# The value products of four quadrants in one TensorE stage, with constants, loads, early experts and a planner's table re-ordered

## The chip, the cores and the metric

The kernel runs on one core of a Trainium2 chip. The metric is device time in microseconds (us) for one execution; lower is better. Five engines work side by side and each takes its instructions strictly in the order of its own list: PE (TensorE, matrix products), DVE (VectorE), ACT (ScalarE), POOL (GpSimd) and SP, which here only issues transfers. POOL issues transfers too.

## What is computed

First a two-part attention over q, k, v of shape 8 x 8 heads x 576 x 64; then its output, as 4608 rows of 512, goes through a mixture of 8 experts, of which every row takes the one with the largest gate.

```python
# attention: a coarse part on means over 4 positions, and a local part
q_d, k_d, v_d = (t.reshape(B, H, S // 4, 4, D).mean(axis=3) for t in (q, k, v))
out_up = np.repeat(sm_attn(q_d, k_d, v_d), 4, axis=2)
mask = np.abs(pos[:, None] - pos[None, :]) < 4
out_local = softmax(np.where(mask, scale * q @ k.T, -1e9)) @ v
x = (out_up + out_local) as rows [4608, 512]
# experts
e_idx = argmax(x @ w_gate, axis=1); gate_w = the largest softmax value
eom = sigmoid(x @ w_output_gate)
out[row] = gate_w[row] * eom[row, e] * (relu(x[row] @ w1[e]) @ w2[e])   # e = e_idx[row]
```

## The kernel before, in words

**Attention.** The work is cut into 32 head pairs (8 batches of 4 pairs), called units `u`. Each runs the same stages: `prep` transposes q and k on PE (L450) and multiplies them with scaled identities for the means (L457, with `idq` and `idk`); DVE and ACT take the results out of PSUM (`qT` L465, `qd` L471, `kT` L478, `kd` L485). `vm` makes the means of v on PE (L497). `scores` does the coarse scores `ms` (L515), a mask product (L524) and the local scores `ls` (L533, 48 small products), then one exponential on ACT (L539), the only one of that line, so that 32 runs of L539 count the units. `values` makes numerators and denominators `uden` (L558, L560, L563), a logarithm and an exponential on ACT (L570, L572), the normalised local weights `en` on POOL (L574), `um` on DVE (L582), and then the local values `val` on PE (L596): 24 products for quadrants 0 and 1 of the sequence into one PSUM pair, then 24 for quadrants 2 and 3 into another. A float32 product stands in the trace as two rows, so a unit has 96 rows of L596. DVE adds both parts into `xT` (L604), POOL casts them (L609).

**Gate.** After each batch `gate` works out the expert and the slot of every row (L641 to L738), and six indirect transfers from POOL scatter the rows into `hx_xs`, sorted by expert (L758).

**Experts.** Each expert has 5 tiles of 128 rows. A `unit` of one or two tiles loads its rows (L808), transposes them (`xgT`, L818, copied by DVE at L822), multiplies with w1 (`up`, L835), applies relu on ACT or DVE (L787, L789), multiplies with w2 (`down`, L850), scales on ACT (L858) and scatters to the output (L792). A two-tile unit has 32 rows of L835 and 16 of L850. `EARLY` names units that may run while attention still goes on: for each of experts 0 to 3 a two-tile unit once the rows of batches 0 to 3 are scattered, and a one-tile unit after batch 5, 12 tiles in all; 28 tiles come after the last batch.

**What sets the order.** Every stage is a task with an engine, a duration, dependences and a priority. `Plan.emit` takes the tasks by earliest start in its own model and writes them out; the engines' lists are the order in which it took them. Wrong durations in that model can't break the result, only make a list wait: `ldv` is planned with 0.06 us on SP, for instance. The constants (L359 to L426) are written out ahead of all tasks. PSUM has four pairs of banks: banks 0 and 1 (`r_T`) for `prep`, `vm` and the gate, three pairs (`r_P`) for scores, `uden` and `val`, and early experts share banks 7 and 6 (`r_Y`) with them; late experts may use all eight (`r_A`).

**First loads.** POOL issues q and k for half a batch (2 units) at a time (L291), SP issues v in 8 transfers of 48 KB for a unit (L320), and 8 fills of `hx_xs` (L869).

Of the kernel before, what the change touches and what calls it, by code (L numbers as in the profile page):

```python
# [16 lines left out]
NGB = 6  # L17
# [6 lines left out]
NJ = 6  # L24
CAPJ = 5
EARLY = {0: ((3, 2), (5, 1)), 1: ((3, 2), (5, 1)), 2: ((3, 2), (5, 1)), 3: ((3, 2), (5, 1))}
LATE_ORDER = (0, 4, 1, 5, 2, 6, 3, 7)
W_AT = (2, 6, 10, 14, 22)
NBLK = 27
Q_AHEAD = 7  # L30
# [8 lines left out]
    "exp_pe": 60.0, "exp_ev": 40.0, "wt": 0.0,  # L39
}  # L40
# [29 lines left out]
class Task:  # L70

    def __init__(self, eng, dur, fn, deps, uses, prio, mode, lat, cost, name):
        self.eng, self.dur, self.fn, self.deps = eng, dur, fn, deps
        self.uses, self.prio, self.mode, self.lat = uses, prio, mode, lat
        self.cost, self.name = cost, name
        self.begin = self.end = self.done = None


class Plan:

    HOP = 0.2
    SWITCH = 0.1

    def __init__(self):
        self.tasks = []
        self.fixed = {}
        self.log = []
        self.dma = 0.0
        self.owner = {}
        self.seen = {}  # L90

    def add(self, eng, dur, fn, deps=(), uses=(), prio=0.0, mode=None, lat=0.0, cost=0.0, name=""):
        t = Task(eng, dur, fn, [d for d in deps if d is not None], list(uses), prio, mode, lat, cost, name)
# [4 lines left out]

    def emit(self, run=True):
        free, mode = {}, None  # L100
        todo = {}
        for t in self.tasks:
            todo.setdefault(t.eng, []).append(t)
        for eng in todo:
            todo[eng].sort(key=lambda t: t.prio)
        n = len(self.tasks)
        while n:
            best = None
            for eng, ts in todo.items():
                here = None  # L110
                at0 = free.get(eng, 0.0)
                for t in ts:
                    s = self.start(t, at0, mode)
# [10 lines left out]
            k, s, t = best  # L124
            if t.mode is not None:
# [3 lines left out]
            t.begin, t.end = s, s + t.dur  # L129
# [5 lines left out]
            todo[t.eng].remove(t)  # L135
            for b in t.uses:
                if b.tile is None:
                    if isinstance(b.ring, Banks):
                        b.banks = self.choose(b, t)[1]
                        for x in b.banks:  # L140
                            self.owner[x] = b
                        b.tile = b.ring.view(b.banks) if run else True
                    else:
# [6 lines left out]
            if run:  # L150
                t.fn()
# [4 lines left out]
    def start(self, t, at, mode):  # L156
        for d in t.deps:
            if d.done is None:
                return None
            at = max(at, d.done + (self.HOP if d.eng != t.eng else 0.0))  # L160
        for b in t.uses:
            if isinstance(b.ring, Banks):
                if b.tile is not None and not b.ring.psum:
                    continue
# [838 lines left out]
```

## Time and profile before

| | |
|---|---|
| median of 3 runs | 593.38 us (584.59 to 598.02) |
| the profiled execution | 592.64 us, its span 590.9 us |
| mean granted TensorE clock | 0.837 of full speed |
| PE busy | 470.2 us (80% of the span) |
| DVE, ACT, POOL busy | 174.7, 142.9, 184.7 us |
| data moved | 65.18 MB, mean 110 GB/s |

The span runs from the first to the last instruction of the profiled execution, which was 592.64 us long. Busy time of PE is read with care: products are pipelined, and the end of each is modelled.

### The profile page before, as it was taken

The numbers are of one execution on the slowest core, as the hardware profiler recorded it, in microseconds if no ns is written. First come the engines' busy times: TensorE is split into PE (matmuls) and PEld (weight loads), VectorE is DVE, ScalarE is ACT, GpSimd is POOL, SyncE is SP. The second block draws the span as 40 slices with busy tenths as digits, with TensorE's granted clock in tenths as the row PEclk, the third lists the DMA queues.
The fourth block names the chain that finished last, engine by engine and source line by source line (L and its number), as shares of the span: only waits on it lengthen the run. The fifth ranks groups of instructions, "written<-read, shape, count | busy, mean of one in ns | idle before, by whom it ended". The sixth has DMA issues, their size and how long they took to land.

```text
span 590.9 us, 22803 instructions
## 1 busy us (share of the span) xinstructions
PE 470.2 (80%) x10283; PEld 364.3 (62%) x10283; DVE 174.7 (30%) x480; ACT 142.9 (24%) x297; POOL 184.7 (31%) x240
## 2 busy tenths in 40 slices
PE   0269987798989968898888788898876878998882
PEld 0157866676877856776757465776754555565651
DVE  3022224313322431532623243225252122131220
ACT  1013122212222222232233322222221222323220
POOL 7002231621532442431442226213424322222211
PEclk9999978557565686767799999658799999999997
DMA  4966997497577574645476356552413584222211
GB/s 55 168 182 111 212 212 121 91 150 111 110 117 126 123 122 82 129 73 119 97 140 145 72 101 119 121 93 33 84 42 116 99 175 109 87 88 81 81 59 55
DMA packets 96430, 65.18 MB, mean 110 GB/s; under 512 B 60737, under 2 KB 88385, under 8 KB 96324
## 3 DMA queue, kind: packets, MB, share of 16 engines
q0 software_dynamic: 31136, 40.43, 36.7%
q1 hardware_dynamic: 65188, 23.20, 17.9%
q8 instruction: 83, 1.36, 1.0%
q14 instruction: 23, 0.19, 0.1%
HBM read 70.33 MB, written 20.53 MB: 154 GB/s over the span
## 4 chain that ended last, share of the span: by engine, by line
PE 71%; issue 9%; DVE 6%; DMA 5%; ACT 5%; POOL 1%; SPq 1%; DVEq 0%; POOLq 0%; ACTq 0%
PE P L835 12%; PE P L850 11%; PE P L596 10%; PE P L558 7%; PE P L563 6%; PE P L450 5%; PE P L457 5%; PE P L497 4%; DMA v<-in_v_dram 3%; PE P L641 2%; PE P L748 2%; ACT hs L787 2%; DVE kT L478 1%; PE P L515 1%; PE P L533 1%
## 5 line engine op out<-in xcount | busy, mean ns | idle before, releaser
L835 PE MATMUL P<-xgT,blk 128*128 128x256 f16 (+1 forms) x768 | 80.0, 256 | 25.1 <-ACT hs L787 11.1
L835 PEld LDWEIGHTS <-blk 128*128 128x128 f16 x768 | 65.0, 98 | 38.0 <-issue 30.4
L850 PE MATMUL P<-blk,hs 128*128 128x512 f16 x320 | 75.1, 379 | 7.9 <-DVE hs L789 4.4
L792 POOL DMA_INDIRECT out_dram<-y,xg x40 | 39.8, 995 | 121.3 <-ACT y L858 117.2
L596 PE MATMUL P<-en,v 32*64 32x24 f32 x3072 | 68.8, 241 | 5.9 <-issue 5.9
L596 PEld LDWEIGHTS P<-en,v 32*64 32x64 f32 x3072 | 62.8, 168 | 15.9 <-issue 13.7
L574 POOL TENSOR_TENSOR en<-e,r 128x288 f32<-128x288 f32 x32 | 25.3, 792 | 120.8 <-issue 72.5
L850 PEld LDWEIGHTS <-hs 128*128 128x128 f16 x320 | 30.5, 98 | 42.3 <-issue 7.2
L450 PE MATMUL P<-id,blk 72*64 72x72 f16 x1024 | 39.8, 238 | 19.1 <-DMA blk<-in_q_dram 11.0
L758 POOL DMA_INDIRECT hx_xs<-xh,g_pos x48 | 45.1, 939 | 31.5 <-DVE g_ohc L708 18.4
L789 DVE TENSOR_SCALAR hs<-P 128x512 f16<-128x512 f32 x40 | 27.7, 692 | 89.7 <-PE P L835 71.2
L609 POOL CAST x<-xT 128x576 f16<-128x576 f32 x32 | 21.3, 666 | 103.6 <-DVE xT L604 86.1
L604 DVE TENSOR_TENSOR xT<-P,u 128x288 f32<-128x288 f32 x64 | 28.9, 455 | 78.1 <-PE P L596 77.5
L558 PE MATMUL P<-e,vd 64*64 64x72 f32 (+1 forms) x512 | 48.2, 351 | 3.6 <-issue 2.2
L450 PEld LDWEIGHTS <-blk 72*64 72x64 f16 x1024 | 32.4, 143 | 27.9 <-issue 15.0
L560 PE MATMUL P<-e,on_d 64*64 64x72 f32 (+1 forms) x512 | 48.6, 351 | 0.0
L858 ACT ACTIVATE y<-P,xg 128x512 f32<-128x512 f32 x40 | 26.8, 686 | 87.6 <-PE P L850 71.7
L497 PE MATMUL P<-v,pv 128*32 128x192 f32 x256 | 28.8, 429 | 21.8 <-DMA v<-in_v_dram 15.2
L558 PEld LDWEIGHTS P<-e,vd 64*64 64x64 f32 x512 | 41.3, 193 | 6.8 <-issue 1.9
L478 DVE COPY kT<-P 128x576 f16<-128x576 f16 x32 | 24.2, 756 | 64.4 <-PE P L457 41.4
L560 PEld LDWEIGHTS P<-e,on_d 64*64 64x64 f32 x512 | 41.7, 193 | 1.2 <-issue 1.2
L563 PE MATMUL P<-e,on_b 128*128 128x144 f32 x128 | 37.8, 441 | 3.2 <-issue 3.2
(118 smaller groups left out, 565.0 us busy)
## 6 DMA issues: line engine op xcount, KB each, us to landing
blk<-in_moe_w_dram POOLq DMA_DIRECT2D x32, 512.0 KB
v<-in_v_dram SPq DMA_DIRECT2D x254, 48.0 KB
hx_xs<-zt SPq DMA_DIRECT2D x8, 645.0 KB
blk<-in_q_dram POOLq DMA_DIRECT2D x15, 288.0 KB
blk<-in_k_dram POOLq DMA_DIRECT2D x15, 288.0 KB
xg<-hx_xs SPq DMA_DIRECT2D x16, 258.0 KB
xg<-hx_xs SPq DMA_DIRECT2D x8, 129.0 KB
hx_xs<-xh,g_pos POOLq DMA_INDIRECT x48
```

The costliest lines, as they stand in the source:

```text
L450: nc.tensor.transpose(t16[64 * h:64 * h + 64, c:c + HB], v_qk(src.tile)[:, h0 + h, a:a + D], id16[0:HB, 0:HB])
L457: nc.tensor.matmul(t32[64 * h:64 * h + 64, c:c + nw], lhsT=v_qk(src.tile)[:, h0 + h, a:a + D], rhs=(idq if i == 0 else idk), start=(m == 0 ...
L478: nc.vector.tensor_copy(kT.tile[:, 4:4 + S].rearrange("p (n j m) -> p n j m", j=2, m=4), T.tile.bitcast(F16)[:, 0:S].rearrange("p (m j n) ...
L497: nc.tensor.matmul(T.tile[r0:r0 + 32, 0:3 * D], lhsT=pv, rhs=vbuf.tile[:, s::2, h, :], start=True, stop=True, skip_group_check=True)
L558: nc.tensor.matmul(p[r, 1, LC + q0:LC + q0 + w], lhsT=vd.tile[r, blk, :], rhs=et[r, i, c0:c0 + w], start=(blk == 0), stop=(blk == 2), skip ...
L560: nc.tensor.matmul(p[rr, 0, DL - SD + q0:DL - SD + q0 + w], lhsT=on_d[r, :], rhs=et[r, i, c0:c0 + w], start=(blk == 0), stop=(blk == 2), s ...
L563: nc.tensor.matmul(p[:, h, DL * (1 - h):DL * (1 - h) + LC], lhsT=on_b, rhs=et[:, h, 0:LC], start=True, stop=True, skip_group_check=True)
L596: nc.tensor.matmul(p[64 * h:64 * h + 64, i, c:c + 24], lhsT=vbuf.tile[r, g, h, :], rhs=et[r, h, 24 * g:24 * g + 24], start=True, stop=True ...
L758: ins = nc.gpsimd.indirect_dma_start(out=xs_dram.ap(), out_offset=bass.IndirectOffsetOnAxis(ap=pos()[:, j:j + 1], axis=0), in_=xh.tile[:, ...
L792: ins = nc.gpsimd.indirect_dma_start(out=out, out_offset=bass.IndirectOffsetOnAxis(ap=idx, axis=0), in_=yt, in_offset=None, bounds_check=N ...
L835: nc.tensor.matmul(o, lhsT=v_w(wb[c // 2].tile, 0)[:, c % 2, 128 * f:128 * f + 128], rhs=xgT.tile[:, c, 0:nt], start=(c == 0), stop=(c == ...
L850: nc.tensor.matmul(py.tile, lhsT=hs.tile[:, f, 128 * j:128 * j + 128], rhs=v_w(wb[2 + f // 4].tile, 2)[:, f % 4, :], start=(f == 0), stop= ...
```

## The change

1. **`val` as one stage.** The 48 products of a unit now go through all four quadrants in turn (0, 2, 1, 3) and write two PSUM pairs, which the stage holds both at once, out of three.
2. **`prep`.** `idk` shrinks from 96 to 72 columns; the blank columns of `kd` are now zeros written once.
3. **Loads.** v comes in 4 transfers of 96 KB for a unit, with the same 256-byte packets. The first q and k loads and the first v loads are issued ahead of most constants, which have become tasks with dependences.
4. **Experts.** `EARLY` is now one two-tile unit for each of experts 0 to 3 after batch 5: 8 tiles, then 32 late ones. Early units may use all eight banks, and 5 buffers instead of 3 hold loaded rows. Weights are asked for later (`W_AT`).
5. **The planner.** It has other durations (two for PE, at either clock level), a table `ADJ` added to the priorities, and a model of the clock. Where its plan has PE wait, `fill` puts products of `ones` with itself into the waiting stage's own PSUM bank.

```diff
-EARLY = {0: ((3, 2), (5, 1)), 1: ((3, 2), (5, 1)), 2: ((3, 2), (5, 1)), 3: ((3, 2), (5, 1))}
+EARLY = {0: ((5, 2),), 1: ((5, 2),), 2: ((5, 2),), 3: ((5, 2),)}
-W_AT = (2, 6, 10, 14, 22)
-NBLK = 27
-Q_AHEAD = 7
+W_AT = (8, 12, 16, 20, 26)
+NBLK = 26
+Q_AHEAD = 5
...
+ADJ = {
+    "down": 2.96, "en": -2.72, "exp": 16.74, "g": -35.07, "gc": -11.68, "gl": -3.33, "gr": -16.35,
...
+            if t.eng == "PE" and self.filler is not None and self.filler.done is not None:
+                fill = self.fill(t, s, max(free.get("PE", 0.0), picks[0], self.filler.done + self.HOP))
...
-    r_Y = Banks([(7,), (6,)], bank1)
+    r_Y = Banks([(x,) for x in (7, 6, 5, 4, 3, 2, 1, 0)], bank1)
...
-    r_xg = ring(sb, [128, 2, XW // 2], I32, "xg", 3)
+    r_xg = ring(sb, [128, 2, XW // 2], I32, "xg", 5)
...
-        for h in range(2):
-            for qd in range(4):
...
-                        nc.sync.dma_start(t[32 * qd:32 * qd + 32, :, h, :],
-                                          _ap(s, [[D, 32], [24 * D, NGB], [1, D]], o))
-                ts.append(plan.add("SP", 0.06, fn, uses=[buf], prio=10.0 * (u - 4) + OFF["v_ld"], lat=2.0, cost=0.22,
-                                   name="ldv"))
+        for qx in range(4):
...
+                nc.sync.dma_start(t[32 * qx:32 * qx + 32, n0:n1, :],
+                                  _ap(s, [[D, 32], [96 * D, n1 - n0], [1, D]], o + 96 * D * n0))
...
+            ts.append(plan.add("SP", 0.88, fn, deps=[C["z"]] if u == 0 and qx == 0 else [], uses=[buf], prio=10.0 * (u - 4) + OFF["v_ld"], lat=1.5, cost=0.5,
+                               name="ldv"))
...
-    idk = cst.tile([HB, NGB * 16], F16)
+    idk = cst.tile([HB, HB], F16)
...
+    def const(eng, dur, fn, prio, deps=(), uses=()):
+        return plan.add(eng, dur, fn, deps=deps, uses=uses, prio=-500.0 + prio, name="c")
...
+        C["ones"] = const("DVE", 0.2, lambda: nc.vector.memset(ones, 1.0), 0)
...
+        C["id"] = const("POOL", 0.8, lambda: make_identity(nc, id16), 0)
...
+        Os = [Buf(r_P), Buf(r_P)]
+
+        def fn():
+            et = en.tile
+            for g in range(NGB):
+                for h in range(2):
+                    for qx in (0, 2, 1, 3):
+                        r = slice(32 * qx, 32 * qx + 32)
+                        c = DL * (1 - qx % 2) + 24 * g
+                        nc.tensor.matmul(Os[qx // 2].tile[64 * h:64 * h + 64, qx % 2, c:c + 24],
+                                         lhsT=vbuf.tile[r, NGB * h + g, :], rhs=et[r, h, 24 * g:24 * g + 24],
+                                         start=True, stop=True, skip_group_check=True)
...
+        def dummy(o, n):
+            w = o.shape[1] // 128
+            while n:
+                m = min(n, w)
+                nc.tensor.matmul(o[:, 0:128 * m], lhsT=ones, rhs=_ap(ones, [ones.ap[0], [0, m], [1, 128]]), start=True,
+                                 stop=True, skip_group_check=True)
+                n -= m
```

The planner's table says little by itself, so here is what stands in the engines' lists. On SP, at the start of the program, before the change (`v_122` to `v_125` are the buffers of units 0 to 3):

```order
L405 DMA wg<-in_moe_w_gate_dram 128x4x8
L406 DMA wg<-in_moe_w_output_gate_dram 128x4x8
L413 DMA tok_c<-tok_r 96x1x1
L313 DMA v_122<-in_v_dram 28x64
L314 DMA v_122<-in_v_dram 32x5x64
L320 DMA v_122<-in_v_dram 32x6x64 x7
L320 DMA v_123<-in_v_dram 32x6x64 x8
```

and after it (`v_120` and so on are now these buffers):

```order
L398 DMA v_120<-in_v_dram 32x12x64 x3
L398 DMA v_120<-in_v_dram 32x11x64
L401 DMA v_120<-in_v_dram 28x64
L398 DMA v_121<-in_v_dram 32x12x64 x4
L398 DMA v_122<-in_v_dram 32x12x64 x4
L398 DMA v_123<-in_v_dram 32x12x64 x4
L525 DMA wg<-in_moe_w_gate_dram 128x4x8
```

Unit 0's v is complete after 5 issues instead of 12, and the small transfers for the gate have gone behind the v of four units.

On PE, the end of the local scores of one unit and the value products of another, before:

```order
L533 LDWEIGHTS kT_120
L533 MATMUL P_94<-qT,kT_120 32x24
L596 MATMUL P_93<-en,v_123 64x24 x24
L596 MATMUL P_92<-en,v_123 64x24 x24
L450 LDWEIGHTS blk_68
```

and the same stage after the change:

```order
L595 LDWEIGHTS blk_67
L595 MATMUL P_90<-idk,blk_67 64x72
L735 MATMUL P_91<-en,v_120 64x24
L735 MATMUL P_93<-en,v_120 64x24
L735 MATMUL P_91<-en,v_120 64x24
L735 MATMUL P_93<-en,v_120 64x24
L735 MATMUL P_91<-en,v_120 64x24
```

Two runs of 24 into one pair each have become one run of 48 that changes the pair at every product. As before, `ms` of the next unit, and mostly its `ls`, stand ahead of a unit's value products.

On SP, where the rows of experts (`xg`) are loaded among the last v transfers, before:

```order
L808 DMA xg<-hx_xs 128x2x258 x3
L320 DMA v_122<-in_v_dram 32x6x64 x8
L320 DMA v_123<-in_v_dram 32x6x64 x8
L320 DMA v_124<-in_v_dram 32x6x64 x8
L808 DMA xg<-hx_xs 128x2x258
L320 DMA v_125<-in_v_dram 32x6x64 x8
L320 DMA v_122<-in_v_dram 32x6x64 x8
L808 DMA xg<-hx_xs 128x258 x2
L320 DMA v_123<-in_v_dram 32x6x64 x8
L320 DMA v_124<-in_v_dram 32x6x64 x8
```

and after:

```order
L398 DMA v_120<-in_v_dram 32x12x64 x4
L398 DMA v_121<-in_v_dram 32x12x64 x4
L950 DMA xg<-hx_xs 128x2x258
L398 DMA v_122<-in_v_dram 32x12x64 x4
L398 DMA v_123<-in_v_dram 32x12x64 x3
L398 DMA v_123<-in_v_dram 32x11x64
L403 DMA v_123<-in_v_dram 28x64
L950 DMA xg<-hx_xs 128x2x258 x4
L950 DMA xg<-hx_xs 128x258
```

The early units have moved from among the last nine units of attention to its very end: on PE the first `xgT` now stands ahead of the last-but-one `uden`, and the scores of the last unit behind it. Of `ones` the PE list holds 30 products with 13,824 columns: 9,600 ahead of the first `prep`, 1,152 and 768 ahead of the next two, 640 in the middle of attention, 1,664 behind the early units. In the late experts the first four `up` products of the next unit now stand ahead of the last `down` products of a unit, and the transposes of the unit after it among them.

## Rows read from the trace of the kernel before

**Rows 1.** The page's 40 slices: granted clock in tenths of full speed (9: 90% or more).

```profile
PEclk9999978557565686767799999658799999999997
```

**Rows 2.** Stage table: length, busy us (rows) of five engines, granted clock, DMA share, GB/s.

```profile
0.00:40.27 40.27, 10.78 (x222) 7.04 (x224) 7.08 (x42) 3.33 (x8) 11.52 (x32) 1.00 0.77 120
40.27:100.05 59.78, 51.80 (x1485) 43.88 (x1484) 17.38 (x44) 15.33 (x36) 15.68 (x22) 0.93 0.91 176
100.05:288.01 187.96, 161.49 (x4533) 136.32 (x4534) 63.62 (x188) 45.69 (x108) 65.93 (x84) 0.64 0.63 112
288.01:375.21 87.20, 71.77 (x1706) 52.21 (x1707) 30.34 (x81) 25.00 (x51) 33.92 (x40) 0.98 0.58 118
375.21:417.86 42.65, 39.14 (x1057) 32.21 (x1053) 14.71 (x44) 10.69 (x27) 12.71 (x16) 0.62 0.39 73
417.86:454.80 36.94, 26.58 (x458) 19.55 (x458) 12.08 (x37) 7.65 (x14) 12.43 (x15) 0.94 0.29 73
454.80:579.40 124.60, 108.44 (x848) 73.07 (x849) 28.80 (x44) 34.49 (x55) 31.53 (x33) 1.00 0.37 99
```

**Rows 3.** The exponentials, one for a unit: count, duration in ns, first and last start.

```profile
L539 ACT ACTIVATE e<-P x32: 770/770/790, 40.3 to 417.9; 128x720 f32<-128x720 f32 x32
```

**Rows 4.** Timeline of the start: start, us, engine, line, idle before and its releaser.

```profile
6.96 1.68 POOL L291 DMA_DIRECT2D blk<-in_q_dram  x2
9.46 27.18 SPq L320 DMA_DIRECT2D v<-in_v_dram  x31
11.03 0.69 PE L450 MATMUL P<-id,blk 72*64 72x72 f16 x16 [11.03 <-DMA blk<-in_q_dram]
18.66 0.85 PE L497 MATMUL P<-v,pv 128*32 128x192 f32 x4 [6.46 <-DMA v<-in_v_dram]
37.24 0.69 PE L450 MATMUL P<-id,blk 72*64 72x72 f16 x16 [0.92 <-DVE kT L478]
```

**Rows 5.** Timeline: single PE stages, of uden, val, ls and prep, at two places.

```profile
51.85 1.33 PE L563 MATMUL P<-e,on_b 128*128 128x144 f32 x4
312.39 0.76 PE L563 MATMUL P<-e,on_b 128*128 128x144 f32 x4
53.11 2.42 PE L596 MATMUL P<-en,v 32*64 32x24 f32 x96
309.29 1.60 PE L596 MATMUL P<-en,v 32*64 32x24 f32 x96
314.18 0.56 PE L533 MATMUL P<-qT,kT 64*32 64x24 f16 x48
37.68 0.89 PE L457 MATMUL P<-idk,blk 72*64 72x96 f16 x16
26.19 0.73 PE L457 MATMUL P<-idq,blk 72*64 72x72 f16 x16
```

**Rows 6.** Waits from 100 to 288 us: who waited, total us, times, longest.

```profile
PE P L533 <- issue: 7.3, 5, 3.4
PE P L596 <- issue: 2.9, 3, 1.9
```

**Rows 7.** Late experts: two stages of one unit, and PE's waits there over the span.

```profile
500.05 3.72 PE L835 MATMUL P<-xgT,blk 128*128 128x256 f16 x32 [0.78 <-DVE xgT L822]
503.61 3.62 PE L850 MATMUL P<-blk,hs 128*128 128x512 f16 x16
PE P L835 <- ACT hs L787: 11.1, 16, 0.7
```

**Rows 8.** The stage table for L850 alone (PE, PEld): 8 rows are one tile.

```profile
288.01:375.21 87.20, 15.26 (x64) 6.20 (x64) 0.98 0.58 118
454.80:579.40 124.60, 51.60 (x224) 21.59 (x224) 1.00 0.37 99
```

**Rows 9.** The stage table for L596 alone: 96 rows are one unit.

```profile
100.05:288.01 187.96, 34.99 (x1536) 32.09 (x1536) 0.64 0.63 112
```

**Rows 10.** The page's costliest groups: busy us, mean ns, idle before and releaser.

```profile
L604 DVE TENSOR_TENSOR xT<-P,u 128x288 f32<-128x288 f32 x64 | 28.9, 455 | 78.1 <-PE P L596 77.5
```

More of the change, by code (lines that the diff above doesn't have):

```diff
@@ L39 @@
     "exp_pe": 60.0, "exp_ev": 40.0, "wt": 0.0,
+}
+ADJ = {
[3 rows of a table added]
+    "prepk": -11.4, "prepq": -2.7, "qT": 9.99, "qd": -37.26, "relu": -45.46, "rex": 52.83, "row": -52.17,
+    "scat": -46.43, "uden": -10.67, "um": 48.9, "up": 2.65, "val": -16.57, "vd": 58.16, "vm": 1.78,
+    "x": 51.76, "x16": 5.26, "xgT": -20.52, "xgTe": 35.12, "y": -16.59,
 }
@@ L128, in emit @@
                 mode = t.mode
-            t.begin, t.end = s, s + t.dur
+            d = t.dur
+            if t.eng == "PE" and t.slow is not None:
+                y = t.stream[0]
+                if not self.state(s):
+                    d, y = t.slow, t.stream[1]
+                self.stream(s, d, y)
+            t.begin, t.end = s, s + d
             t.done = t.end + t.lat
@@ L134, in emit @@
             free[t.eng] = t.end
-            todo[t.eng].remove(t)
+            ready[t.eng].remove(t)
+            for x in later.get(t, ()):
+                need[x] -= 1
+                if not need[x]:
+                    ready[x.eng].append(x)
+            new = None
             for b in t.uses:
@@ L150, in emit @@
             if run:
+                if fill:
+                    if t.spare is not None:
+                        self.dummy(t.spare(), fill)
+                    else:
+                        o = new.tile
+                        self.dummy(o[:, 0, :] if len(o.shape) == 3 else o, fill)
                 t.fn()
@@ L358, in consts @@
+    C = {}
     def consts():
[L359 to L369 removed]
@@ new lines, in consts, with fn @@
+        C["idq"] = const("DVE", 0.45, fn, 2, [C["id"]])
+        def fn():
+            for t in pool_kT + pool_kd:
+                nc.vector.memset(t, 0.0)
+        C["kz"] = const("DVE", 0.7, fn, 3)
+        p4 = pv[:, 0:24].rearrange("p (j a i) -> p j a i", j=2, a=4)
+        def fn():
+            t = p4[0:32, :, 0, :]
+            nc.gpsimd.memset(t, 0.25)
+            for cm, base in ((1, -4), (-1, 7)):
+                nc.gpsimd.affine_select(out=t, in_=t, compare_op=ALU.is_ge, fill=0.0, base=base,
+                                        pattern=[[-4 * cm, 2], [-8 * cm, 3]], channel_multiplier=cm)
@@ new lines, in consts, with fn @@
+        c = const("POOL", 0.6, fn, 500 - 39.9, [C["z"]])
+        def fn():
+            for a in range(1, 4):
+                nc.vector.tensor_copy(p4[32 * a:32 * a + 32, :, a, :], p4[0:32, :, 0, :])
+        C["pv"] = const("DVE", 0.6, fn, 5, [c])
+        def fn():
+            nc.gpsimd.memset(mb, 0.0)
+            for cm, base in ((1, -1), (-1, 7)):
+                nc.gpsimd.affine_select(out=mb, in_=mb, compare_op=ALU.is_ge, fill=-8192.0, base=base,
+                                        pattern=[[-cm, 4], [-4 * cm, 2], [-8 * cm, 3]], channel_multiplier=cm)
@@ new lines, in consts, with fn @@
+        c = const("POOL", 0.6, fn, 500 - 39.9, [c])
+        def fn():
+            nc.vector.tensor_copy(mk[64:96, 0, 0:24], mk[0:32, 0, 0:24])
+            nc.vector.tensor_copy(mk[64:96, 2, LC - 24:LC], mk[0:32, 2, LC - 24:LC])
+        C["mk"] = const("DVE", 0.4, fn, 7, [c])
+        def fn():
+            nc.vector.memset(on_b, 0.0)
+            for a in range(4):
+                nc.vector.memset(on_b[32 * a:32 * a + 32, 32 * a:32 * a + 32], 1.0)
+            nc.vector.tensor_reduce(on_c, id16.rearrange("p (a i) -> p a i", i=32)[:, :, 0:24], axis=AX.XY, op=ALU.add)
+            nc.vector.tensor_copy(on_d, _bc(on_c[:, 0], 64))
```

365 lines of the change are left out of this document (207 added, 158 removed), and 2 rows, old and new, of the table ADJ.

## The prediction

> **What bounds the kernel now.** I read the clock line of the page first, then a table of stages cut at the exponentials, then timelines of single stages. The 32 runs of L539 mark the units: the first starts at 40.27 us, the last at 417.86 [rows 3]. They cut the span of 590.9 us in three: a start of 40.27, attention of 377.6, and an end of 173.0 (417.86 to 590.9).
>
> In the start PE is busy for 10.8 of 40.27 us [rows 2]. The first `prep` begins at 11.03, 4.07 us after POOL issued the first q, and the first `vm` waits for v until 18.66 [rows 4]. SP spends 27.18 us on 31 v transfers, 0.877 us each, so the seventh of them, with which unit 0's v is complete, is issued by 15.6, and `vm` starts 3.1 us later. The PE list puts the `vm` of four units ahead of the first k, so nearly all of PE stands behind SP's issues.
>
> In attention PE is the bound, at a low clock. From 100.05 to 288.01, 1536 rows of L596 are 16 units [rows 9], so a unit takes 11.75 us; PE is busy for 161.5 of 188.0 us, at a mean granted clock of 0.64 [rows 2]. [...]
>
> By L850, 64 rows or 8 early tiles stand inside attention, and 28 tiles in the late stage of 124.6 us [rows 8]: 4.45 us for a late tile. Its products alone need less: a two-tile unit has 3.56 us from the start of `up` to that of `down`, then 3.62 [rows 7], and with 0.5 for its transposes (my allowance) 7.7, so 3.9 for a tile. Between the last exponential and the late stage lie 36.94 us with PE busy for 26.6 and four early tiles in it [rows 2].
>
> **The change, part by part.** Base: attention without its 8 tiles is 377.6 - 8 x 3.9 = 346.4 us. By 40.27 PE had also done preps and `vm`s for units to come; 8 us for that (10.8 us of busy rows, less unit 0's own) gives 354, or 11.4 us a unit, near the 11.75 read directly.
>
> *Start.* The first q is issued after the identity at 1.4 us or so instead of 6.96, and 4.07 later (5.5) `prep` may begin; k comes two issues later. Unit 0's v needs 5 issues of 0.88 from about 0.9, so 5.3, and the same 3.1 more: 8.4. From the last k `prep` to the exponential the old start took 3.0 us (37.24 to 40.27) [rows 3, 4]. First exponential: about 12. [...] Bounds: 10 if nothing queues, 27 if all first loads (3.3 MB of q, k and v, by shape) must arrive at the start's 120 GB/s [rows 2]; I stay near the low end, since the list asks for unit 0's data first.
>
> [...]
>
> *`val`.* 96 rows take 2.42 us at one place and 1.60 at another, with 4 array tiles in turn (2 row groups by 2 heads) [rows 5]. The nearest row with 8 tiles in turn is L533: 48 rows in 0.56, with the last row's length in it. [...] Bounds: 0 (rows come no faster) and 1.2.
>
> [...]
>
> *`prep`.* 16 products of 96 columns took 0.89 us, of 72 columns 0.73 [rows 5]; 0.13 a unit at the mix of levels. Zeros for `kd` are written once, on DVE, busy for a third of the stretch; without that cover 0.3 us in all.
>
> *Clock.* L596 is 35.0 of 161.5 us of PE's busy time [rows 2, 9]; with it halved, and stalls fewer, I expect the mean to rise from 0.64 to about 0.75. [...] I take -0.7. [...]
>
> *Waits.* 26.5 us of the stretch PE is idle, 1.65 a unit. The largest is "issue", a wait for nothing that the trace shows: 7.3 us ahead of L533 alone, 3.4 at most [rows 6], all such rows 1.0 a unit. That stays. Of the other 0.65, part goes with v's SP time (7.0 us of issues a unit becomes 3.5) and with truer durations: -0.35, between 0 and 0.65. A wait is added: `val` needs two of three PSUM pairs, and the `uden` and scores behind it on PE need one back, after two adds of 0.455 [rows 10]. I count 0, since `uden` (over 1.5 us) stands between.
>
> A unit then takes 11.4 - 1.0 - 0.13 - 0.7 - 0.35 = 9.2 us, and 31 of them 285.
>
> *End.* The early tiles move here: 40 tiles instead of 32. After the last exponential I count 8 us for the rest of attention and the last gate, 40 tiles, and 11.5 us for the last scatter and the closing code (579.4 to 590.9). The old hole of 10 idle us in 36.94 is covered by about 18 us of early tiles. A tile: 4.15, between 3.9 (no waits) and 4.45 (as now): with `up` of the next unit ahead of the last `down`, about half of the waits, such as 11.1 us for relu [rows 7], have work under them. 8 + 166 + 11.5 = 185.5, 12.5 more than before.
>
> *Sum.* 12 + 285 + 185.5 = 482.5 of span, and 1.7 around it (592.64 - 590.9): 484 us. The execution read was 592.64, the median of the runs 593.38, so no correction.
>
> **The rivals.**
> 1. *Clock and waits don't improve.* For it: full speed between 288 and 375 us, at 0.98, came with expert tiles mixed in, which attention loses. Against it: `val` shrinks anyway. 10.3 us a unit, 319 us: 518.
> 2. *Four quadrants come no faster.* `val` saves 0, the clock half as much: about 10.7 a unit, 332: 531. For it: every product has weights of its own to load; against it the row of L533.
> 3. *Clock mostly at the upper level.* The unit would fall below 8.3, but attention moves about 45 MB (the four stages' lengths by their GB/s, less the early tiles, plus first loads that shift), and at the 176 GB/s of the busiest stage [rows 2] that is 256 us. With 181 at the end: 451. Transfers then are the bound.
> 4. *The other side: PSUM pairs run out.* If the scores of the next unit wait behind `val` for a pair, PE stands for two adds (0.9), the scores (1.1) and the exponential (0.77), 2.9 with gaps, in each unit, and gains nothing in clock: 13.2 us, 409: 608. It decides from 12.7 us a unit on. Against it: `ms` of the next unit stands ahead of `val` in the list.
>
> **How the numbers follow.** Forecast (465 to 505): 0.49. Rival 1 (505 to 525): 0.22. Rival 2 (525 to 545): 0.10. Rival 3 (445 to 465): 0.13. Rival 4, and parity close to it: 0.06. Predicted 484; the range of 450 to 535 leaves out rival 4, half of rival 2 and the low edge of rival 3. A change of about 2% can be told from none here. All cases but the last are over 8% faster: faster 0.93, same 0.03, slower 0.04.
>
> **What would show it.** First L539 at 10 to 16 us, v issues over by 16. Rows of `val`: 96 in 1.1 to 1.3 us; above 1.5 rival 2 holds. A clock of 0.70 to 0.80 between the sixth unit and the last; near 0.6 it is rival 1. Last L539 at about 297; above 400 rival 4. Late tiles at 4.0 to 4.3, no hole of PE ahead of them. DMA share over 1 through attention would speak for rival 3. I am wrong most easily in the clock: it is the largest term without a row of its own.

## The result, and the profile after

The changed kernel takes 547.27 us (median of 4 runs, 545.31 to 549.12) against 591.05 for the kernel before (584.59 to 598.02): a ratio of 0.933, 95% interval 0.925 to 0.941. (Where the runs of a kernel fall into a faster and a slower state, ratios here use the faster runs alone, so this one is not that of the two medians.) I had said 484, with a range of 450 to 535. The direction held and the size did not: the gain is 44 us where I forecast 109. The execution read has a span of 543.5 us, 545.2 with the 1.7 around it. The experiments below ran in several groups; in some of them the kernel before took 593 us and in others 637, so times are compared only within a group or by their ratio to the kernel before.

First the granted clock of the page (its 40 slices), then the stage table, cut at the first and last exponential (length, busy us and rows of PE, PEld, DVE, ACT, POOL, granted clock, DMA share, GB/s), and the exponentials themselves:

```profile
PEclk8555787568857556556765785869999999999997
```

```profile
0.00:17.80 17.80, 12.19 (x228) 7.11 (x230) 7.34 (x39) 2.62 (x6) 14.11 (x32) 0.80 1.07 156
17.80:362.40 344.60, 277.40 (x8563) 228.43 (x8563) 118.42 (x343) 86.46 (x205) 116.90 (x149) 0.66 0.69 125
362.40:400.00 37.60, 34.06 (x487) 24.48 (x485) 15.09 (x40) 10.50 (x19) 17.73 (x20) 1.00 0.41 102
```

```profile
L679 ACT ACTIVATE e<-P x32: 770/770/791, 17.8 to 362.4; 128x720 f32<-128x720 f32 x32
```

Against [rows 2, 3] the start went from 40.27 to 17.8 us, attention from 377.6 to 344.6, and the end from 173.0 to 181.1. Start and end are near the forecast (12 and 185.5). Attention is not: 11.1 us a unit where I had 9.2. Its clock is 0.66, not 0.75, and PE stands still for 67.2 us of it, 2.17 a unit.

What PE waits for in attention (who waited, for what, total us, times, longest):

```profile
PE P L735 <- issue: 20.6, 12, 3.8
PE P L698 <- issue: 9.9, 5, 3.9
PE P L673 <- issue: 7.5, 4, 3.2
PE P L595 <- issue: 5.0, 3, 3.0
PE P L588 <- ACT vd L641: 2.5, 4, 1.3
```

The four largest rows are "issue", the wait for nothing that the view shows. All such rows sum to 52 us here, against 28 in attention before, where the two largest were

```profile
PE P L533 <- issue: 8.6, 6, 3.4
PE P L596 <- issue: 5.9, 9, 1.9
```

This is where the forecast was lost, so the longest of these waits is worth a closer look: PE's timeline (start, us, idle before) just behind it, and the transfer queues in the 3 us ahead, in two pieces, 166 to 169 and 169 to 171 (queue: packets, MB, share of 16 engines).

```profile
173.07 0.50 PE L698 MATMUL P<-e,vd 64*64 64x144 f32 x1 [3.85 <-issue]
```

```profile
q0 software_dynamic: 214, 0.22, 67.5%
...
q0 software_dynamic: 312, 0.30, 94.1%
q1 hardware_dynamic: 497, 0.12, 28.2%
q8 instruction: 1, 0.02, 3.0%
```

PE stands from 169.22 to 173.07. From 167 to 171 the transfer engines are full with an expert's weights (q0, from POOL) and v (q1, from SP). The one packet of queue q8, an instruction block of 16,384 bytes, starts only at 170.85, as q0 runs dry; it has landed at 171.8, and PE goes on 1.25 us later. There are 83 such blocks in the trace, as many as before, for 20,626 rows of PE (weight loads and products), so about 250 rows to a block. And PE's unexplained waits lie at fixed distances: ahead of its rows 953, 1460, 1971, 2480, 3245 and 3754, to name the first six of attention. Counted with the 102 other instructions in PE's list (semaphores, mostly), 20,728 in all, these distances are 512, 512, 512, 768 and 512: twice or three times 256, exactly. My estimate from these distances is 256 instructions to a block, and so 64 bytes each (16,384 / 256).

Below, a **stop** is this: PE idle (neither a product nor a weight load running) for 0.4 us or more, ending 0.9 to 2.0 us behind the landing of a block. In attention the kernel before has 20, 26.5 us in all; the changed kernel 29, 53.1 us. By place, 26 of these 29 (51.3 us) and 19 of the 20 (25.8 us) stand exactly at a step from one 256 instructions to the next. All other idle time of PE fell, from 25.9 to 13.2 us. Of the 26 stops over 0.7 us, 20 have 2.5 us or more of other transfers (their time over 16 engines) in the 4.8 us around the start of their block; of the 39 blocks without a stop 19 do, so by itself this says little.

The clock fell in this stop. The stage table around it:

```profile
164.30:169.20 4.90, 4.80 (x250) 3.84 (x244) 2.49 (x11) 1.98 (x5) 1.56 (x2) 1.00 0.47 54
169.20:173.10 3.90, 0.05 (x6) 0.03 (x4) 1.27 (x7) 0.55 (x3) 0.00 (x0) 0.75 0.99 170
173.10:212.00 38.90, 35.06 (x897) 29.54 (x900) 12.79 (x31) 9.12 (x20) 16.75 (x22) 0.50 0.67 119
```

In the traces of both kernels every entry of the clock's record is 1.00 or 0.50 of full speed. The clock was 1.00 ahead of the stop, fell during it (0.75 over its 3.9 us), and stayed at 0.50 for the next 39 us, with PE busy for 35 of them. Of the 16 falls in attention, 12 lie in a stop or within 1.6 us behind one, where some 4 would by chance (26% of the time at 1.00 lies there); in the kernel before it is 4 of 12, with 2 by chance. So stops are one cause of falls, probably, and not the only one. What keeps the clock down afterwards is not shown: the first 24 of these 39 us hold no other stop.

### The profile page after: what moved, and what is told of

The parts are those of the page before. It is cut to its first block, busy times and chain, and to the rows that moved or that the text cites. A ratio compares the mean times of both kernels' runs of the same rounds, so it can differ in the third digit from the quotient of the medians.

```text
span 543.5 us, 22586 instructions
## 1 busy us (share of the span) xinstructions
PE 449.5 (83%) x10313; PEld 345.8 (64%) x10313; DVE 175.3 (32%) x477; ACT 141.7 (26%) x297; POOL 187.8 (35%) x242
## 4 chain that ended last, share of the span: by engine, by line
PE 79%; issue 11%; DVE 5%; ACT 2%; POOL 0%; POOLq 0%; DVEq 0%; ACTq 0%
PE P L994 13%; PE P L978 13%; PE P L735 9%; PE P L698 8%; PE P L703 6%; PE P L588 6%; PE P L595 4%; PE P L637 4%; PE P L890 3%; PE P L783 3%; PE P L655 2%; PE P L673 2%; PE P L960 2%; PE P L1065 2%; DVE xh L894 1%
## 5 line engine op out<-in xcount | busy, mean ns | idle before, releaser
L978 PE MATMUL P<-xgT,blk 128*128 128x256 f16 (+1 forms) x768 | 77.6, 255 | 6.3 <-ACT y L1003 2.6
L994 PE MATMUL P<-blk,hs 128*128 128x512 f16 x320 | 76.4, 379 | 1.1 <-DVE hs L931 0.7
L735 PE MATMUL P<-en,v 32*64 32x24 f32 x3072 | 50.9, 254 | 21.0 <-issue 20.6
L735 PEld LDWEIGHTS P<-en,v 32*64 32x64 f32 x3072 | 45.4, 175 | 29.7 <-issue 26.5
L698 PE MATMUL P<-e,vd 64*64 64x72 f32 (+1 forms) x512 | 50.3, 356 | 10.3 <-issue 9.9
L700 PE MATMUL P<-e,on_d 64*64 64x72 f32 (+1 forms) x512 | 50.8, 356 | 0.5 <-issue 0.5
L698 PEld LDWEIGHTS P<-e,vd 64*64 64x64 f32 x512 | 42.6, 196 | 11.3 <-issue 8.9
L746 DVE TENSOR_TENSOR xT<-P,u 128x288 f32<-128x288 f32 x64 | 26.9, 452 | 62.8 <-PE P L735 49.8
L588 PE MATMUL P<-id,blk 72*64 72x72 f16 x1024 | 36.2, 226 | 8.6 <-ACT kd L625 3.6
L588 PEld LDWEIGHTS <-blk 72*64 72x64 f16 x1024 | 29.4, 133 | 20.0 <-issue 15.9
L710 ACT ACTIVATE r<-P 128x432 f32<-128x432 f32 x32 | 17.0, 530 | 94.4 <-PE P L703 94.4
```

What stands on the lines that cost most here:

```text
L588: nc.tensor.transpose(t16[64 * h:64 * h + 64, c:c + HB], v_qk(src.tile)[:, h0 + h, a:a + D], id16[0:HB, 0:HB])
L698: nc.tensor.matmul(p[r, 1, LC + q0:LC + q0 + w], lhsT=vd.tile[r, blk, :], rhs=et[r, i, c0:c0 + w], start=(blk == 0), stop=(blk == 2), skip ...
L700: nc.tensor.matmul(p[rr, 0, DL - SD + q0:DL - SD + q0 + w], lhsT=on_d[r, :], rhs=et[r, i, c0:c0 + w], start=(blk == 0), stop=(blk == 2), s ...
L735: nc.tensor.matmul(Os[qx // 2].tile[64 * h:64 * h + 64, qx % 2, c:c + 24], lhsT=vbuf.tile[r, NGB * h + g, :], rhs=et[r, h, 24 * g:24 * g + ...
L746: nc.vector.tensor_tensor(xT.tile[:, hp, 2 * SD * ph:2 * SD * ph + 2 * SD].rearrange("p (g m c) -> p g m c", m=4, c=6), _ap(o, [o.ap[0], [ ...
L978: nc.tensor.matmul(o, lhsT=v_w(wb[c // 2].tile, 0)[:, c % 2, 128 * f:128 * f + 128], rhs=xgT.tile[:, c, 0:nt], start=(c == 0), stop=(c == ...
```

## The experiments

The theory that comes out of this, D: instruction blocks (each 256 of PE's instructions, by the estimate above) wait behind data, PE stops, and a stop takes the clock down. Rivals: one stream alone is to blame (A: v's; B: that of POOL), the waits have nothing to do with data (C), the clock is set by PE's own columns, or the order or the early experts are the cause. E adds to D why the change made more stops: faster rows use a block up sooner.

The changed kernel unaltered, in two groups of the longer times:

> The changed kernel unaltered, on the chip and between the runs of the kernel before that the other runs of this group share: 0.93 of the kernel before again, waits for nothing shown 50 to 60 us in attention, granted clock there 0.64 to 0.70.

> The changed kernel unaltered, as the measure for the two runs with the spread fill and for the stops: 0.93 of the kernel before, stops of 50 to 62 us.

Measured 0.934 [0.924, 0.943] and 0.943 [0.938, 0.947], with 59.1 and 52.4 us of stops in attention. So ratio and stops are much the same in both kinds of group. (By place alone these two have 54.3 and 47.1 us; in groups marked * the definition also catches some other waits.) The table has the runs in the order told; * marks groups in which the kernel before took 637 us; length, clock and stops are those of attention. Where the clock's record begins late, its mean is from that time on. Each row is one trace, and the mean clock of single runs of the changed kernel goes from 0.758 to 0.803 over the whole span.

| run | length, us | clock | stops, us | ratio to before, or times of its runs |
|---|---|---|---|---|
| before / after | 377.6 / 344.6 | 0.74 (from 74.2 us) / 0.66 | 26.5 / 53.1 | 1 / 0.933 |
| after* (two runs) | 391.3, 387.7 | 0.64, 0.62 | 59.1, 52.4 | 0.934, 0.943 |
| no v* | 377.9 | 0.66 | 49.4 | - |
| no v, q, k* | 347.1 | 0.73 | 35.5 | - |
| no v, q, k, weights | 297.1 | 0.76 | 27.1 | - |
| before, four quadrants* | 401.9 | 0.73 (from 61.8 us) | 46.6 | 0.996 |
| two quadrants* | 389.8 | 0.65 | 43.2 | 0.949 |
| no ones* | 389.8 | 0.68 (from 46.4 us) | 61.6 | 592.9 to 606.7 us |
| more ones* | 390.3 | 0.70 | 56.7 | 0.948 |
| no order table* | 378.8 | 0.65 | 42.5 | 598.5 to 611.9 us |
| early experts as before | 375.2 | 0.76 | 60.5 | 0.978 |
| loads in halves* | 387.1 | 0.65 | 61.7 | 0.943 |
| halves, paced | 350.6 | 0.74 | 48.8 | 552.0 to 564.4 us |
| fill spread* | 380.0 | 0.66 | 43.9 | 0.948 |
| fill spread, q and k in halves* | 372.3 | 0.67 | 40.4 | 0.928 |

**Taking transfers away.** In `load_v`, `load_qk` and `weights`:

```diff
+                if u >= 4:
+                    return
                 s = v[b, 2 * hp]
...
+                    if b > 0:
+                        nc.gpsimd.memset(v_qk(bufs[i].tile)[:, h0:h1, :], 0.0)
+                        return
                     s = src[b, half * HP + h0:half * HP + h1]
...
+                if e < len(W_AT):
+                    nc.gpsimd.memset(o, 0.0)
+                    return
                 if i < 2:
```

> The loads of v are left out for units 4 to 31 (SP's list keeps its places, empty); these units work on the v of units 0 to 3. In the changed kernel PE waits 53.7 us in all for nothing that the trace shows, and the last exponential begins at 362.4. Theory A (PE's instructions arrive in blocks of 16,384 bytes over the same transfer engines as the data, and a block that stands behind data stops PE; v's bursts are most of it): those waits fall to 20 to 30 us, the last exponential comes at 325 to 335, and with fewer stops the granted clock in attention rises to 0.70 or more. Theory B (the same, but q, k, weights and scatters of POOL's queue are what blocks stand behind): waits 45 or more, last exponential 350 to 360. Theory C (the waits have nothing to do with data): 50 to 55 us, 358 to 363.

> As the run without v, and q and k of batches 1 to 7 are replaced by zeros that POOL writes; weights, gates and experts stay. Theories A and B: the waits for nothing shown fall under 15 us in attention. If the granted clock follows the stops, it rises from 0.66 to 0.75 or more there and the last exponential begins at 290 to 305; if the clock is set by PE's own work and not by the stops, it stays at 0.64 to 0.68 and the last exponential comes at 315 to 330. Theory C: waits 50 us or more, last exponential after 350.

> The loads of v (units 4 to 31), of q and k (batches 1 to 7) and of the five experts' weights that fall into attention are left out (zeros by POOL for q, k and weights); the zero fill, scatters and gates stay. Theory D (stops are instruction blocks waiting behind data, and the clock falls because of stops): from the eighth unit on hardly a stop of 0.9 us or more at a block's boundary (under 8 us in all), granted clock in attention 0.8 or more behind the first 70 us, last exponential at 260 to 300. If the clock does not follow the stops: no stops, clock 0.64 to 0.70, last exponential at 315 to 330. Theory C (stops have nothing to do with data): stops of 40 us and more remain.

Only attention is read here: without these loads the rows of the experts change, and the end, 352 to 361 us, is not comparable. Without v the stops stay at 49.4 us: theory A falls. Without q and k too they are 35.5, and the last exponential comes at 367.6 us (405.7 and 409.5 in the two controls): more stops than A and B said, fewer than C, and a later last exponential than A and B had. Without the weights as well, attention is 297.1 us, the stage table's row (as above) and the largest waits for nothing shown are

```profile
19.70:316.80 297.10, 250.90 (x8561) 209.47 (x8561) 119.60 (x351) 86.44 (x205) 161.63 (x149) 0.76 0.18 45
```

```profile
PE P L740 <- issue: 4.3, 5, 1.2
PE P L678 <- issue: 3.9, 3, 2.7
```

(the second view from the eighth unit on). Against the changed kernel, in a group whose kernel before agrees with its own within 0.4%, the same PE work takes 47.5 us less: 26 fewer in stops and 26.5 fewer in busy time, at 0.76 instead of 0.66, while other idle time grew by 4.9. So C falls, and D holds in kind for the stops. For the clock it is less clear: in both of these runs with a higher clock (0.73 and 0.76) q and k are zeros, and whether PE's clock rises for that alone was not tried. D's numbers were too bold: I expected under 8 us of stops from the eighth unit on, a clock of 0.8 and the last exponential by 300. From the eighth unit on 17.3 us remain (39.6 with data), nearly all 0.4 to 1.4 us long and most with no data in flight (the DMA share of this attention is 0.18, not 0.69). In attention as a whole the stops of 1.5 us and more went from 39.4 us to 8.9. So two things are mixed: long stops behind data, and short ones where PE uses up 256 instructions faster than a block can come, even over idle queues. That time can be put together from this trace: a block's packet starts 1.0 us (median) behind PE's step into the block ahead of it, takes 0.9 to 1.5, and PE goes on no sooner than 1.2 behind its landing, so some 3.1 to 3.7 us by my estimate from these figures.

**Faster rows.** The kernel before with one edit, the four quadrants in one stage (its planner must also pick two PSUM pairs at once), and the changed kernel with its quadrants in the order of before:

```diff
-        for ph in range(2):
-            O = Buf(r_P)
+        Os = [Buf(r_P), Buf(r_P)]
...
-                    for i in range(2):
-                        r = slice(64 * ph + 32 * i, 64 * ph + 32 * i + 32)
+                    for qx in (0, 2, 1, 3):
+                        r = slice(32 * qx, 32 * qx + 32)
```

> The kernel before with one edit of the change: the values of a unit in one stage of four quadrants in turn. Its 96 rows at 1.1 to 1.8 us instead of 1.6 to 2.4, about 0.6 a unit. Theory E (PE's faster rows use up an instruction block sooner, and so more blocks come too late): stops of 0.4 us and more with a block just landed go from 29.5 us (24 of them) to 40 to 55, and the kernel is only 0 to 10 us faster than before. If the change's other parts make the stops: stops 25 to 33 us, the clock in attention 0.64 or higher, and the kernel 18 to 30 us faster.

```diff
-            for g in range(NGB):
-                for h in range(2):
-                    for qx in (0, 2, 1, 3):
+            for qs in ((0, 1), (2, 3)):
+                for g in range(NGB):
+                    for h in range(2):
+                        for qx in qs:
```

> One stage and both PSUM pairs as in the changed kernel, but the 96 rows go through quadrants 0 and 1 first and then 2 and 3, as the kernel before did. If products of four quadrants in turn are what made the stage shorter (2.15 us a unit before, 1.59 after): 2.0 to 2.3 us a unit again, and the time 12 to 22 us longer. If it was the single stage: still 1.5 to 1.7 us and no difference in time.

The stage table for the values' rows alone (PE, PEld), the kernel before with the edit, and then the kernel before without (from the other kind of group):

```profile
0.00:616.30 616.30, 50.71 (x3072) 44.71 (x3072) 0.82 0.52 106
```

```profile
0.00:590.90 590.90, 68.81 (x3072) 62.79 (x3072) 0.84 0.56 110
```

The stage gave some 18 us, and the kernel gained nothing: 0.996 [0.991, 1.001] within its group. Its stops are 46.6 us instead of 26.5. That is what theory E says: what PE saves in rows comes back as waiting for the next block. Alone this run does not prove it. The two traces are from different kinds of group (the changed kernel's own rows take 50.9 us in one and 64.0 in the other), this one is of the fastest of 12 runs (618.1 us, median 631.1), and the planner also put other tasks in another order. PE's list itself says more. Cut into blocks of 256 instructions, it shows how long PE took for each, idle time left out, and whether a stand of 0.4 us or more followed:

| attention of | blocks under 3.5 us | with a stand behind | blocks of 3.5 us or more | with a stand behind |
|---|---|---|---|---|
| before | 17 | 9, 11.3 us | 51 | 10, 14.5 us |
| after | 31 | 20, 38.8 us | 36 | 6, 12.4 us |
| no v, q, k, weights | 39 | 21, 23.1 us | 27 | 1, 1.6 us |

The change made quickly used blocks nearly twice as many, and the added stops lie behind them; with data on the queues such a stop is longer. The other way round, the slower order in the changed kernel costs 15.7 us of rows (79.6 instead of 64.0 in its group's control) and has 9 to 16 us fewer stops; the time is 602.9 against 598.4 and 598.9 in groups whose kernel before agrees within 0.3%, so some 4 us of the 12 to 22 that I expected, and the intervals of the ratios overlap (0.949 [0.942, 0.955]).

**The clock by itself.** The products of ones left out, and four more of 128 columns behind each unit's values:

```diff
-        plan.filler = C["ones"]
...
+            for i in range(4):
+                nc.tensor.matmul(Os[i // 2].tile[:, i % 2, LC:LC + 128], lhsT=ones, rhs=ones, start=True, stop=True,
+                                 skip_group_check=True)
```

> No products of ones in PE's planned waits. Of 30 such products in the changed kernel 24 lie in the first 18 us and 6 behind. If they hold the clock up for attention: granted clock below 0.64 in attention, time 8 us or more longer. If they do nothing after the start: clock 0.65 to 0.68, time within 3 us of the changed kernel.

> [...] If denser columns bring the clock up: granted clock in attention 0.72 or more against 0.66, and the kernel 5 to 30 us faster than the changed kernel. If stops and waits, not columns, hold the clock down: clock 0.64 to 0.68, 7 to 13 us slower.

With more ones neither expectation was met whole. The trace has a clock of 0.70, and the time went from 0.934 to 0.948 (intervals that just overlap): PE was busy for 291.8 us with them and 292.7 without, so the faster clock paid for the added columns and no more. Without any, the clock was 0.68 from 46.4 us on, where its record begins, and the time 592.9 to 606.7 us, not to be told from the 591.0 to 602.7 of the changed kernel in other groups: as expected if they do nothing after the start. So ones in PE's waits neither carry the kernel nor explain the missing clock; 24 of the changed kernel's 30 lie in its start.

**Order and early experts.** The table of shifts at zero, and `EARLY`, `W_AT` and `Q_AHEAD` of the kernel before:

```diff
-        t = Task(eng, dur, fn, [...], list(uses), prio + ADJ.get(name, 0.0), mode, ...
+        t = Task(eng, dur, fn, [...], list(uses), prio, mode, ...
...
-EARLY = {0: ((5, 2),), 1: ((5, 2),), 2: ((5, 2),), 3: ((5, 2),)}
-W_AT = (8, 12, 16, 20, 26)
-Q_AHEAD = 5
+EARLY = {0: ((3, 2), (5, 1)), 1: ((3, 2), (5, 1)), 2: ((3, 2), (5, 1)), 3: ((3, 2), (5, 1))}
+W_AT = (2, 6, 10, 14, 22)
+Q_AHEAD = 7
```

> The table of shifts that orders the tasks is left out (all zero), all else as in the changed kernel. If the order is what spreads transfers and fills PE's waits: real waits of PE on ACT, DVE and POOL in attention rise from about 15 us to 40 or more, and the kernel is 15 to 60 us slower than the changed kernel. If the order does not matter: within 6 us.

> Early experts, their weights' places and the lead of q and k as in the kernel before: 16 tiles in 12 steps, 8 of them in attention, weights from the second unit on. The end term of the prediction (40 tiles in the end instead of 32): with 32 tiles there the end is 15 to 25 us shorter and attention 25 to 35 us longer; over all 0 to 15 us slower than the changed kernel. If weights, q, k and v that come closer together are what makes more stops in the changed kernel: stops at boundaries 10 us or more fewer than in the changed kernel, and the time equal or up to 10 us faster.

Without the table the kernel takes 598.5 to 611.9 us, its control 591.0 to 602.7: the ranges overlap, so a difference is not shown, least of all the 15 to 60 us that I expected if the order matters. Real waits rise (5.8 us on one bitmap of the gate, 5.8 on kT), but stops fall to 42.5, so its attention is even shorter, by 12.5 us, while its end is 16.4 longer (207.8 to 191.4). With the early experts as before the kernel is 0.978 [0.954, 1.003], some 27 us slower than the changed one: attention longer by 30.6, as expected, the end shorter only by 5.0 where I expected 15 to 25. (The edit gives 12 early tiles in 8 steps, as in the kernel before, not the 16 in 12 that I put down.) Stops are 60.5, so the later place of the weights is not what made them more. Of what was taken out of the change, this part cost the most. And with so many stops the clock of its attention is 0.76, not 0.66:

```profile
18.70:393.90 375.20, 293.75 (x8720) 230.37 (x8721) 126.19 (x352) 96.40 (x222) 123.10 (x155) 0.76 0.67 124
```

So stops alone do not set the level of the clock; the expert tiles in this attention are the likely reason, as in the kernel before (0.98 where its early tiles lie, [rows 2, 8]).

**Moving transfers.** If D and E hold, the same bytes in shorter bursts should help. Four tries: q, k and weights in halves at places of their own; the same with a POOL operation behind each load; the zero fill of the expert rows on ACT in 24 pieces; this with q and k in halves.

```diff
-        pieces = [(0, 2), (2, 4)] if (b, half) == (0, 0) else [(0, 4)]
+        pieces = [(0, 2), (2, 4)]
...
-            weights(e, 10.0 * w0 + OFF["wt"], [[st[w0 + i]["exp"]] for i in range(4)])
+            weights(e, 10.0 * w0 + OFF["wt"], [([st[w0 + i]["exp"]], [st[w0 + i]["x16"]]) for i in range(4)])
```

> The loads of weights, q and k on POOL's queue are cut in halves (288 or 256 packets a load become 144 or 128 to 256), each half issued at a place of its own between POOL's two operations of a unit; the same bytes. Theory D (an instruction block waits behind whatever data stands ahead of it on the transfer engines, and stops PE when that is over some 3 us of transfers): the stops of 0.9 us and more at block boundaries fall from about 50 us in all to 25 or less, and the kernel is 15 to 40 us faster than the changed kernel, more if the clock follows. Theory C (the stops have nothing to do with data): within 5 us of the changed kernel, stops as before.

```diff
+                    nc.gpsimd.tensor_tensor(scr, scr, scr, op=ALU.mult)
```

> The halves of the run with cut loads, and behind each of POOL's loads in attention a product of 256 columns that nothing reads, some 0.7 us, so that two loads are issued 1.5 us apart and not 0.75; the same bytes. Theory D: the stops at block boundaries fall from 65 us to 35 or less, as a queue no longer builds up; POOL's values for `val` come up to 3 us later in units with several loads, so waits of PE on POOL rise by 10 to 30 us; the time within 15 us of the run with cut loads, either side. Theory C: stops as before, 55 us and more, and the time 10 to 30 us longer.

```diff
-            nc.sync.dma_start(
-                xs_dram.ap()[r * REG:r * REG + 128 * CAPJ, :]...
+        for i, (j, n) in enumerate(((0, 2), (2, 2), (4, 1))):
+                nc.scalar.dma_start(
+                    xs_dram.ap()[r * REG + 128 * j:r * REG + 128 * (j + n), :]...
```

> The changed kernel, with the zero fill of the expert rows cut from 8 transfers of 645 KB on SP's queue to 24 of 129 and 258 KB, each issued by ACT behind one of its six operations of a unit, over the first four units; all else as it is. In the changed kernel four stops between 38 and 72 us of the record (8.5 us in all) have 2.0 to 4.5 us of the fill's packets ahead of the block. Theory D: those four stops shrink to 3 us or less in all, the clock rises before 55 us, and the first eight units are 8 to 15 us shorter; the kernel 4 to 12 us faster than the changed kernel. Otherwise within 3 us.

> As the run with the spread fill, and q and k of two pairs come in two transfers each at places of their own instead of one (288 packets become 2 times 144). Theory D: first exponential at 13.5 to 15.5 instead of 17.8, since the first halves alone stand ahead of the first unit; stops 5 to 15 us fewer than with the spread fill alone; the kernel 5 to 20 us faster than the changed kernel. If halves that are issued right behind each other make the same burst: only the start's 3 us.

Three of the four missed outright. Halves gave 61.7 us of stops and no time: POOL has two places a unit between which it issues, and my reading, not tried further, is that both halves still ended up side by side with other loads. Paced, stops were 48.8 where I expected 35 or less, and the time 552.0 to 564.4 us in a group whose kernel before took 582.0 to 596.0, not better than the changed kernel. The spread fill took the early stops (34 to 76 us) from 8.8 to 6.9 us instead of under 3, left the first eight units at 89.0 us (90.4 in the control), and the kernel no faster.

The last beats both kernels: 588.6 us (583.8 to 594.1) against 598.4 (597.4 to 601.2) for the changed kernel in the same group, 0.928 [0.923, 0.934] of before. Its trace is of its fastest run, 583.8 us. Control first (both stages from first to last exponential):

```profile
18.00:405.70 387.70, 297.34 (x8562) 244.35 (x8563) 118.30 (x343) 86.58 (x205) 120.74 (x153) 0.62 0.61 112
```

```profile
14.20:386.50 372.30, 280.75 (x8487) 228.48 (x8495) 121.90 (x350) 85.68 (x205) 137.72 (x181) 0.67 0.63 113
```

The first exponential comes 3.8 us earlier, as expected, and attention is 15.4 us shorter: 12 fewer in stops, 16.6 fewer busy at the higher clock, 13.4 more in other waits. The end is 4.7 longer. Against the spread fill alone its stops are only 3.5 us fewer, where I expected 5 to 15, so that part missed too. Why this pair of edits gains time when each with other company gave none is open.

## Why the prediction was wrong, and where it was right

**Start, 12: measured 17.8.** Five rows of the timeline:

```profile
1.12 5.56 PE L1065 MATMUL P<-ones 128*128 128x512 f16 x19 [1.12 <-DVE ones L444]
6.61 0.45 PE L588 MATMUL P<-id,blk 72*64 72x72 f16 x16
9.91 0.48 PE L1065 MATMUL P<-ones 128*128 128x512 f16 x2 [0.94 <-ACT qd L610]
11.90 0.87 PE L637 MATMUL P<-v,pv 128*32 128x192 f32 x8 [0.67 <-issue]
17.56 0.20 PE L673 MATMUL P<-qT,kT 64*32 64x24 f16 x3 [1.11 <-issue]
```

The ones end at 6.68, and `prep` begins at 6.61, 1.1 later than the 5.5 of the forecast. `vm` began at 11.90 instead of 8.4, since three preps stand ahead of it (6.61, 8.27, 10.33) that wait for evictions of two PSUM banks; from there it is 5.9 us to the exponential, where 12 left 3.6. Of that, 1.11 is the first stop.

**`val`, -1.0 a unit: measured -0.57.** The mechanism was right; single stages of 96 rows:

```profile
80.05 1.15 PE L735 MATMUL P<-en,v 32*64 32x24 f32 x96
179.60 1.71 PE L735 MATMUL P<-en,v 32*64 32x24 f32 x96
263.54 1.79 PE L735 MATMUL P<-en,v 32*64 32x24 f32 x96
```

The first ran at a granted clock of 1.00 in 1.15 us, the others at 0.50 in 1.71 and 1.79. No run shows the 1.0 of the sum: the mean in attention is 1.62 (48.6 us for 2880 rows) against 2.19 in [rows 9]. Rival 2 is out: 1.15 us is 12 ns a row, where the 1.60 us of [rows 5], also at 1.00, are 17. By the sign that I had set (above 1.5 us rival 2 holds) the mean would have spoken for it; the sign had left out the lower clock.

**Clock, -0.7: measured nothing.** 0.66 after 0.64 in the stretch without expert tiles. The step that failed is its reason, "stalls fewer": the stops doubled, and 12 of 16 falls lie at one. That the stops alone kept the clock down is not shown, and the run with early experts as before (0.76) speaks against it, so this part of the cause stays open. No run shows the -0.7 itself. The nearest to it is the run without loads, where at 0.76 the busy time of a unit was 8.09 us, instead of 8.95 at 0.66. And attention as a whole did not start from 0.64 but, as far as the record goes, from 0.74:

```profile
74.20:417.86 343.66, 291.90 (x7889) 235.85 (x7885) 117.56 (x335) 87.68 (x201) 119.60 (x148) 0.74 0.61 114
```

It was at 1.00 from 296.05 to 374.56 us, where the early tiles lie that the change moved out; I had named this under rival 1 and left it out of the sum.

**Waits, -0.35: measured +0.52.** The step that failed is "That stays", said of the issue rows. I read them as a fixed price and did not ask what they were. Real waits did shrink, by more than I counted (other idle time, 25.9 to 13.2 us, 0.4 a unit). But the issue rows are, nearly all of them, stops at instruction blocks. They depend on how fast PE uses up 256 instructions and on what the transfer queues hold; the first went from 17 quick blocks to 31, and the second the change altered too.

**Sum of attention.** 59.6 us too little. Waits: 2.17 - 1.30 = 0.87 a unit, 27 us. Clock: 0.7, 22 us. `val`: 0.43, 13 us. The rest, -2.6, is the base and small terms, so the base (11.4) held as far as the sum can tell.

**End, 185.5: measured 181.1.** (181.1 - 19.5) / 40 = 4.04 a tile, forecast 4.15. As foreseen the hole is gone (34.06 us busy of 37.6), and waits on relu shrank, by the row that answers to the last of [rows 7]:

```profile
PE P L978 <- ACT hs L929: 2.1, 3, 0.7
```

This is for the span as in [rows 7], where 11.1 us stood; of those only 4.2 were in the late stage.

**Rivals.** Rival 1 (clock and waits don't improve, 518) came nearest, and its ground, that attention loses the clock of the expert tiles, fits the rows above; it was still 29 us short, because the waits did not stay but grew. No rival named instruction blocks, so the range ended at 535. Rival 3 (transfers bound the kernel) was right that transfers matter, through another door; a unit below its 8.3 us no run shows, and without the loads it was 9.6 (297.1 / 31). Rival 4 did not happen: no wait of PE on the adds of `val` is among the listed ones.

## What to carry to other kernels

A wait of PE for nothing that the profile shows is not a constant (here such rows went from 28 to 52 us): count PE's instructions between such waits. Where the distances are multiples of 256, as here, ask whether an instruction block comes in the time that PE takes for 256 instructions, beside the data on the same 16 transfer engines (3.1 to 3.7 us for a block, by the estimate above, and up to 3.9 us of standing). Here faster rows then paid only in part or not at all (some 18 us of rows and no time; 15.7 us and some 4). That fewer rows are worth more is a guess of mine that was not tried; shorter bursts gave nothing in three runs of four. Ask of a forecast rise in clock which standstills go away and which dense work leaves the stage: here one stop was followed by 39 us at 0.50, and an attention with as many stops but with expert tiles in it kept 0.76.

## What the hardware did that I had not expected

**Blocks.** In the attention of both kernels an instruction block of 16,384 bytes took 0.9 to 1.8 us once begun, and PE went on 1.2 to 1.9 us behind its end; PE stood still for up to 3.9 us at a boundary, and for 5.6 in the kernel before with four quadrants. The stops cost 26.5 us of 377.6 before and 53.1 of 344.6 after, and behind quickly used blocks they stayed with mostly idle queues too (DMA share 0.18), nearly all at 0.4 to 1.4 us.

**Rows beside POOL's scatters.** In the trace of the last control, of a group marked *, PE slowed to some 10 rows (weight loads and products) in 0.73 us while POOL issued its six scatters of a gate, as in this timeline:

```profile
144.30 0.43 PE L735 MATMUL P<-en,v 32*64 32x24 f32 x5 [0.29 <-issue]
145.05 0.44 PE L735 MATMUL P<-en,v 32*64 32x24 f32 x5 [0.32 <-issue]
145.78 0.44 PE L735 MATMUL P<-en,v 32*64 32x24 f32 x6 [0.29 <-issue]
...
146.13 0.92 POOL L900 DMA_INDIRECT hx_xs<-xh,g_pos  x1 [0.30 <-issue]
147.35 0.92 POOL L900 DMA_INDIRECT hx_xs<-xh,g_pos  x1 [0.30 <-issue]
```

One stage of values takes 9.4 us there (141.85 to 151.25), beside 1.7 elsewhere, and five of the eight batches have a stage of values like it in this trace (6.8 to 9.5 us): it is a likely part, not shown to be all, of the 44 us by which the kernel before differs between groups. In the changed kernel's trace from the other kind of group a stage beside them took 1.68 us (133.07 to 134.75, scatters from 133.60 on). What makes the difference was not tried.
